# A decode kernel of four attention layers: how the transfers and products around a layer's end are ordered

What was changed: the head mapping of the backward layer was mended; the last two heads' rows of `wo` (`wol`) now load into the slot of `wo`'s third block; the five row parts of `wq` in layers 2 and 3 come in groups of 2, 2, 1 instead of 1, 2, 2; V28's products moved ahead of the last softmax; each of the last two heads is evicted in one activation instead of two.

## The chip, the cores and the metric

The kernel runs on one core of one Trainium2 chip. The metric is device time in microseconds (us). Layers are numbered 0 to 3, heads 0 to 31. Times inside a trace count from the span's start. Engines: PE is TensorE, PEld its weight loads, DVE VectorE, ACT ScalarE, SP the engine that issues the transfers. QT names PE's products with parts of `wq`, S the scores, YB the products with `wo`, TB a head's gather (the step that turns its evicted output into columns for `wo`).

## The reference

One token passes through four attention layers, with the weights and caches of A, B, A, B.

```python
for w in (A, B, A, B):           # D = 640, 32 heads, 8192 keys, head size 192, bf16
    q = layernorm(x) @ w.wq      # wq: 640 x 6144
    s = q_h . K_h * 192**-0.5    # K_h, V_h: 8192 x 192 for each head, 3.1 MB each
    o = softmax(s) . V_h
    x = x + concat(o) @ w.wo     # wo: 6144 x 640
```

Each K and V tile is used once per layer, so nearly all of the work is reading 848.4 MB.

## The kernel before

SBUF holds eight slots, each big enough for one K or V tile. A fixed `plan` lists all transfers; SP issues them in that order, and each waits until its slot's last user is done. `steps` is the program order of the computing engines.

```python
Q_PARTS = [[(0, 2), (2, 2), (4, 1)] if l < 2 else [(0, 1), (1, 2), (3, 2)] for l in range(NL)]
KEPT = {0: {("k", 0), ("v", 0)}, 1: {("v", 28), ("v", 29), ("v", 30), ("v", 31)}}   # reused two layers later
...
if l == 2 and p == 0:     # m: score products, s: softmax, v: V products, wq: columns of q
    part = [("m", l, 0), ("wq", l, 1), ("s", l, 0), ("v", l, 0), ("wq", l, 2)]   # ("wq", l, 0) is ahead
...
if p == H - 1:            # end of a layer
    part.append(("s", l, p))
    part += [("v", l, i) for i in range(H - AHEAD, H)]      # V28 to V31
    part.insert(-O_LAST, ("wc", l, 2))
...
plan.append(("wo", l, 2)); plan.append(("wol", l))          # wo's third block, then its last two heads
```

A K tile is multiplied by q in place on DVE, in four chunks; PE adds up the 192 columns with 24 matmuls of 512 columns, and only then is the slot free:

```python
for c in range(4):
    PE.wait(chunks[c])
    for r in range(QD // R):      # 6 matmuls per chunk
        ...matmul(S, lhsT=ident, rhs=k3[:, :, d0:d0 + R])
freed[nt] = ev_S[h] = e
```

The turn from layer 1 to layer 2: V28 to V31 of layer 1 and K0, V0 of layer 0 are kept there, so six of the eight slots are taken. The other two hold K31 and then `wq`'s first part, and `wo`'s third block and then `wq`'s second part. The third part waits until the first has been used; the next K tile, head 1 of layer 2, here called K1, waits until K0's scores are added up.

Of the kernel before, what the change touches and what calls it, by code (L numbers as in the profile page):

```python
# [63 lines left out]
HEADS_W = 10  # L64
# [3 lines left out]
AHEAD = 4  # L68
# [3 lines left out]
def build(nc, A_x, A_k, A_v, A_wq, A_wo, B_x, B_k, B_v, B_wq, B_wo, out):  # L72
# [13 lines left out]
    QW = H * DH  # L86
    Q_PARTS = [[(0, 2), (2, 2), (4, 1)] if l < 2 else [(0, 1), (1, 2), (3, 2)] for l in range(NL)]
    O_PART = [P] * NL
    OI = [O_LAST * DH // n for n in O_PART]
    NB = 3  # L90
    G = 4
# [6 lines left out]
    with ExitStack() as ctx:  # L98
# [14 lines left out]
        oT = sb("oT", [P, NW], BF16)  # L113
        oTl = sb("oTl", [P, max(OI)], BF16)
        o_sb = sb("o_sb", [P, 2 * DH], F32)
# [81 lines left out]
        for l in range(NL):  # L197
            if l < 2:
                plan.append(("wq", l, 0))
                steps += [("wq", l, g) for g in range(3)]  # L200
            elif l == 2:
                plan += [("wq", l, g) for g in range(3)]
                steps.append(("wq", l, 0))
            else:
                plan.append(("wq", l, 0))
                steps.append(("wq", l, 0))
            for p in range(H):
                if p in (HEADS_W, 2 * HEADS_W):
                    b = p // HEADS_W - 1
                    steps += [("wc", l, b), ("wo", l, b)]  # L210
                    plan.append(("wo", l, b))
                if first_load("k", l, p) == ("k", l, p):
                    plan.append(("k", l, p))
                if stays("k", l, p):
                    plan.append(("t", l, p))
                if l == 2 and p == 0:
                    part = [("m", l, 0), ("wq", l, 1), ("s", l, 0), ("v", l, 0), ("wq", l, 2)]
                elif p < H - AHEAD:
                    part = [("m", l, p), ("s", l, p), ("v", l, p)]
                else:  # L220
                    part = [("m", l, p)]
                    if p > H - AHEAD:
                        part.append(("s", l, p - 1))
                    if p == H - 1:
                        part.append(("s", l, p))
                        part += [("v", l, i) for i in range(H - AHEAD, H)]
                        part.insert(-O_LAST, ("wc", l, 2))
                steps += part
                plan += [n for n in part if n[0] == "v" and first_load(*n) == n]
                if l == 3 and p == 1:  # L230
                    for g in (1, 2):
                        plan.append(("wq", l, g))
                        steps.append(("wq", l, g))
            plan.append(("wo", l, 2))
            steps.append(("wo", l, 2))
            plan.append(("wol", l))
            steps.append(("wol", l))
        plan.append(("wob", NL - 1))
        at = {n: i for i, n in enumerate(steps)}

        def released(n):

            if n[0] in "kvt":
                l, p = n[1:]
                if n[0] != "t" and stays(*n):
                    l, p = n[1] + 2, ORDER[n[1] + 2]["heads"].index(head(*n[1:]))
                return at[("v" if n[0] == "v" else "m", l, p)]
            return at[n]
# [15 lines left out]
        for n in plan:  # L264
            if n[0] == "wol" and n[1] + 1 < NL:
                m = ("wq", n[1] + 1, 0)
                allot(m)
                before[n] = before[("wq", n[1] + 1, 2)] if n[1] == 0 else before[m]
            elif n[0] == "wob":
                before[n] = []  # L270
            elif n not in place:
                allot(n)
# [4 lines left out]
        def wq_rows(l, g):  # L277

            c0, k = Q_PARTS[l][g]
            if l < 2:  # L280
                i = place[("wq", l, 0)] * TS
                return pool[:, i + c0 * QW:i + (c0 + k) * QW].rearrange("p (c n) -> p c n", c=k)
            return slot[place[("wq", l, g)]][:, 0:k * QC].rearrange("p (c n) -> p c n", c=k)

        def wol_rows(l):

            if l + 1 == NL:
                i = place[("wol", l)] * TS
            else:
                i = place[("wq", l + 1, 0)] * TS + (DC * QW if l == 0 else QC)  # L290
            return pool[0:O_PART[l], i:i + OI[l] * D]

        def transfer(n):
# [4 lines left out]
            if n[0] == "wol":  # L298
                r0 = o["wol"] * DH
                if O_PART[l] == P:  # L300
                    return SP.op(lambda s: s.dma_start(
                        wol_rows(l), w["wo"][r0:r0 + O_LAST * DH].rearrange("(p i) n -> p (i n)", p=P)),
                        *free, sem=semOL, inc=16)
                k = O_PART[l] // O_LAST
                for h in range(O_LAST):
                    e = SP.op(lambda s, h=h: s.dma_start(
                        wol_rows(l)[h * k:(h + 1) * k],
                        w["wo"][r0 + h * DH:r0 + (h + 1) * DH].rearrange("(q e i) n -> e q (i n)", e=8, i=OI[l])),
                        *free, sem=semOL, inc=16)
                return e  # L310
            if n[0] == "t":
# [13 lines left out]
            elif n[0] == "wq":  # L325
                c0, k = Q_PARTS[l][n[2]]
                f = lambda s: s.dma_start(
# [52 lines left out]
        def layer(l, ev_z, ev_true):  # L380
# [36 lines left out]
            def q_columns(g):  # L417

                n = ("wq", l, g)
                c0, k = Q_PARTS[l][g]  # L420
                t3 = wq_rows(l, g)[:, :, ORDER[l]["q1"] if l < 2 else 0:]
# [16 lines left out]
            def q_spread(h):  # L438

                c0 = h * DH  # L440
                PE.wait(last["qT"], last["QB"], ev_const)
# [15 lines left out]
            def project(n, rows, o, ev_o):  # L457

                t3 = rows.rearrange("p (i n) -> p i n", n=D)
                k = t3.shape[1]  # L460
                end = n == ("wob", l) or n == ("wol", l) and l + 1 < NL
                PE.wait(ev_o, need(n), last["YB"])
                for i in range(k):
                    for c in range(DC):
                        e = PE.op(lambda t, i=i, c=c, f=y_first[0], fin=end and i == k - 1: t.matmul(  # L465
                            YB[:, c:c + 1], lhsT=t3[:, i, c:D:DC], rhs=o[:, i:i + 1], start=f, stop=fin,
                            skip_group_check=True), signal=(i == k - 1 and c == DC - 1), bank=use["YB"])
                        y_first[0] = False
                freed[n] = e
                return e  # L470
# [65 lines left out]
            def values(h):  # L536
# [16 lines left out]
                if h < H - O_LAST:  # L553
                    parts = [(o_sb[:], OB[par][:, 0:2 * DH])]
                else:
                    q = 1 if O_PART[l] == P else O_PART[l] // O_LAST // 8
                    parts = [(o_sb[:, i * DH:(i + 1) * DH].rearrange("p (i e q) -> p q e i", i=OI[l], q=q),
                              OB[par][:, i * DH:(i + 1) * DH].rearrange("p (q e i) -> p q e i", i=OI[l], q=q))
                             for i in range(2)]
                for o, i in parts:  # L560
                    ev_os[h] = AC.op(lambda a, o=o, i=i: a.activation(o, i, ACT.Copy, scale=rl[pi][:, 0:1]),  # L561
                                     e, ev_rl[h], last["osb"], bank=use[f"O{par}"])
                last["O"][par] = last["rl"][pi] = ev_os[h]

            def gather(h):
# [6 lines left out]
                last["osb"] = e  # L572
                o0 = (h % HEADS_W) * DH
                last["TO"] = last["row_written"] = AC.op(
                    lambda a: a.activation(orow[0:1, o0:o0 + DH], TB[0:1, C_O:C_O + DH], ACT.Copy), e, last["orow"], bank=use["TB"])  # L575

            def gather_last(h):

                n = O_PART[l] // O_LAST
                k = OI[l]  # L580
                r0 = (h - (H - O_LAST)) * n
# [14 lines left out]
            for i, n in enumerate(here):  # L596
# [15 lines left out]
                elif n[0] == "wc":  # L612
                    todo()
                    todo = None
                    columns(NW)
                    last["oTw"] = last["TT"]
                elif n[0] == "wo":
# [3 lines left out]
                    k = NW - NB if n == ("wo", NL - 1, 2) else NW  # L621
                    last["oT"] = project(n, slot[place[n]][:, 0:k * D], oT[:, 0:k], last["oTw"])
                else:
                    last["TT"] = last["TTn"]
                    last["oTl"] = ev_y = project(n, wol_rows(l), oTl[0:O_PART[l]], last["TTn"])
                    if l + 1 == NL:
                        ev_y = project(("wob", l), slot[place[("wo", l, 2)]][:, (NW - NB) * D:NW * D], oT[:, NW - NB:NW], last["oTw"])
                following = [m[2] for m in here[i + 1:] if m[0] == "m" and m[2] not in ev_q][:1]
# [68 lines left out]
```

## Time and profile before

| | before |
|---|---|
| device time | 1997.24 us median of 3 (1996.39 to 1998.24) |
| profiled span | 1994.7 us |
| read | 848.4 MB, mean 426 GB/s |
| a 3.1 MB tile follows the last in the stream after | 7.30 us |
| last V tile landed | 1983.18 us |

From the page of the kernel before: busy time, the shares in 40 slices, and the chain that ended last.

```profile
PE 1392.6 (70%) x10438; PEld 318.0 (16%) x7494; DVE 1047.4 (53%) x1074; ACT 220.3 (11%) x665; POOL 4.5 (0%) x22
...
DMA  9999999999999999999999999999999999999998
GB/s 410 431 431 428 432 429 429 430 431 430 428 430 431 428 432 428 431 429 429 431 382 431 428 431 428 431 430 429 431 429 427 430 430 429 430 429 429 429 432 345
...
q8 instruction: 70, 1.15, 0.2%
...
DMA 65%; PE 21%; DVE 12%; ACT 1%; issue 1%; another core or an unknown queue 0%; DVEq 0%
```

The kernel is bound by its transfers. Only the first, the last and slice 21 (382 GB/s) fall clearly below 430 GB/s. Slice 21 is the turn from layer 1 to layer 2. The stretches there, of the kernel before (columns: busy time and count of each engine, granted PE clock, DMA share, GB/s):

```profile
1013.00:1022.00 9.00, 6.88 (x146) 5.89 (x146) 0.35 (x4) 1.41 (x5) 0.00 (x0) 0.92 0.51 213
1022.00:1031.00 9.00, 7.21 (x62) 2.65 (x53) 6.36 (x12) 0.73 (x2) 0.54 (x1) 0.51 0.99 390
1031.00:1040.00 9.00, 8.14 (x137) 3.76 (x125) 2.66 (x5) 0.44 (x2) 0.00 (x0) 0.87 1.03 434
```

There is a hole from 1013 to 1022 us, where the mean DMA share is 0.51. The chain of waits of the kernel before through this stretch (start, us, what; a DMA line runs from a transfer's issue to its landing, the time that it stands in the queue included):

```profile
986.85 30.96 DMA pool<-in_B_wo_dram
1017.81 0.05 issue
1017.86 3.77 PE YB L465 x90
...
1025.52 1.77 DVE pool L495
1027.30 0.05 issue
1027.34 0.61 PE S L508
1027.95 6.42 PE S L58 x23
1034.37 2.23 PE QT L427 x90
...
1040.79 20.01 DMA pool<-in_A_k_cache_dram
```

Layer 2 starts when `wo`'s third block has landed, at 1017.8 us, and its products are done.

### The profile page before, as it was taken

Reading aid. Unit: us, or ns where it says so; the run is one execution under the profiler, and the core shown is the slowest. Engines: PE = TensorE matmul, PEld = TensorE weight load, DVE = VectorE, ACT = ScalarE, POOL = GpSimd, SP = SyncE. Lnnn points to the kernel's source line nnn. Section 1 sums busy time; section 2 is a strip of 40 time slices with the busy share of each in tenths; the row PEclk is TensorE's granted clock in tenths of the full one; section 3 lists DMA queues with packets and bytes.
Section 4 is the critical chain, followed back from the end, with each engine's and each line's share of the span. In section 5 each row is a group of like instructions: output and inputs, shape, how many; then the busy total and the mean of one; then the engine's idle time right before and its main releaser. Section 6 shows DMA issues by size and latency. Waiting matters only on the chain.

```text
span 1994.7 us, 20412 instructions
## 1 busy us (share of the span) xinstructions
PE 1392.6 (70%) x10438; PEld 318.0 (16%) x7494; DVE 1047.4 (53%) x1074; ACT 220.3 (11%) x665; POOL 4.5 (0%) x22
## 2 busy tenths in 40 slices
PE   4777777667567766767777676777776768767766
PEld 1111111111311111211031111111112212111112
DVE  3554554556255455455726545545663465554563
ACT  0111111110111111111011111111101111111111
POOL 0000000000000000000000000000000000000000
PEclk9888888887688888788878878887897888987889
DMA  9999999999999999999999999999999999999998
GB/s 410 431 431 428 432 429 429 430 431 430 428 430 431 428 432 428 431 429 429 431 382 431 428 431 428 431 430 429 431 429 427 430 430 429 430 429 429 429 432 345
DMA packets 40487, 849.67 MB, mean 426 GB/s; under 512 B 4688, under 2 KB 4688, under 8 KB 5328
## 3 DMA queue, kind: packets, MB, share of 16 engines
q1 hardware_dynamic: 40256, 848.38, 99.4%
q8 instruction: 70, 1.15, 0.2%
q14 instruction: 17, 0.14, 0.0%
q10 hardware_dynamic: 144, 0.00, 0.0%
HBM read 848.36 MB, written 0.00 MB: 425 GB/s over the span
## 4 chain that ended last, share of the span: by engine, by line
DMA 65%; PE 21%; DVE 12%; ACT 1%; issue 1%; another core or an unknown queue 0%; DVEq 0%
DMA pool<-in_B_k_cache_dram 32%; DMA pool<-in_A_k_cache_dram 30%; PE S L58 13%; DVE pool L495 10%; PE O L546 3%; DMA pool<-in_B_wo_dram 2%; PE TB L569 1%; DMA x_bf<-in_A_x_dram 1%; PE S L508 1%; PE YB L465 1%; DVE s_sb L516 1%; ACT p_sb L526 1%; PE QT L427 1%; PE TB L530 1%; DVE small L523 0%
## 5 line engine op out<-in xcount | busy, mean ns | idle before, releaser
L495 DVE TENSOR_TENSOR pool<-pool,q_sb 128x3072 bf16<-128x3072 bf16 x512 | 865.5, 1752 | 406.4 <-DMA pool<-in_A_k_cache_dram 208.3
L58 PE MATMUL S<-pool,ident 128*128 128x512 bf16 x2944 | 797.2, 425 | 35.1 <-DVE pool L495 34.9
L546 PE MATMUL O<-pool,p_sb 128*2 128x384 bf16 x4096 | 346.5, 420 | 1.4 <-DMA pool<-in_B_v_cache_dram 1.4
L508 PE MATMUL S<-pool,ident 128*128 128x512 bf16 x128 | 60.4, 472 | 225.7 <-DVE pool L495 225.5
L516 DVE TENSOR_REDUCE s_sb<-S 128x64 f32<-128x512 f32 x128 | 88.3, 690 | 229.1 <-PE S L58 229.1
L546 PEld LDWEIGHTS O<-pool,p_sb 128*2 128x2 bf16 x4096 | 128.0, 88 | 134.8 <-issue 98.4
L569 PE MATMUL TB<-o_sb,small 128*1 128x192 f32 x480 | 122.8, 389 | 38.2 <-DVE small L534 27.1
L453 ACT ACTIVATE q_sb<-QM 128x192 bf16<-128x192 f32 x120 | 39.6, 330 | 961.2 <-PE QM L446 961.2
L446 PEld LDWEIGHTS QM<-ident,qT 128*128 128x128 bf16 x240 | 23.1, 98 | 741.0 <-issue 725.6
L530 PE MATMUL TB<-small,ones 128*128 128x1 f32 x256 | 49.7, 263 | 109.9 <-ACT p_sb L526 109.9
L520 PE MATMUL QM<-ident,m_bf 128*128 128x128 bf16 x128 | 27.8, 217 | 122.9 <-DVE m_bf L519 121.2
L561 ACT ACTIVATE o_sb<-O,small 128x384 f32<-128x384 f32 (+1 forms) x136 | 77.2, 579 | 233.2 <-PE O L546 233.2
L534 DVE RECIPROCAL small<-TB 128x1 f32<-128x1 f32 x128 | 21.5, 168 | 122.4 <-PE TB L530 122.4
L526 ACT ACTIVATE p_sb<-s_sb,small 128x64 bf16<-128x64 f32 x128 | 44.5, 348 | 266.5 <-DVE small L523 266.5
L523 DVE TENSOR_REDUCE small<-QM 128x1 f32<-128x128 f32 x128 | 37.3, 291 | 62.3 <-PE QM L520 62.3
L575 ACT ACTIVATE orow<-TB 1x192 bf16<-1x192 f32 x120 | 38.3, 319 | 200.7 <-PE TB L569 200.7
L530 PEld LDWEIGHTS TB<-small,ones 128*128 128x128 f32 x256 | 38.9, 191 | 130.4 <-ACT p_sb L526 130.4
L508 PEld LDWEIGHTS S<-pool,ident 128*128 128x128 bf16 x128 | 12.7, 99 | 285.8 <-DVE pool L495 285.8
L520 PEld LDWEIGHTS QM<-ident,m_bf 128*128 128x128 bf16 x128 | 12.3, 96 | 215.3 <-ACT q_sb L453 126.9
L569 PEld LDWEIGHTS TB<-o_sb,small 128*1 128x1 f32 x480 | 33.5, 89 | 81.1 <-DVE small L534 36.0
L465 PE MATMUL YB<-oT,pool 128*128 128x1 bf16 x900 | 38.0, 178 | 5.1 <-DMA pool<-in_A_wo_dram 2.3
L465 PEld LDWEIGHTS YB<-oT,pool 128*128 128x128 bf16 x900 | 37.0, 131 | 5.9 <-ACT oT L479 2.9
(50 smaller groups left out, 215.4 us busy)
## 6 DMA issues: line engine op xcount, KB each, us to landing
pool<-in_B_k_cache_dram SPq DMA_DIRECT2D x64, 3072.0 KB, 35.5
pool<-in_A_k_cache_dram SPq DMA_DIRECT2D x63, 3072.0 KB, 27.6
pool<-in_A_v_cache_dram SPq DMA_DIRECT2D x63, 3072.0 KB, 33.3
pool<-in_B_v_cache_dram SPq DMA_DIRECT2D x60, 3072.0 KB, 37.2
pool<-in_A_wo_dram SPq DMA_DIRECT2D x6, 2400.0 KB, 24.0
pool<-in_B_wo_dram SPq DMA_DIRECT2D x5, 2400.0 KB, 33.3
pool<-in_A_wq_dram SPq DMA_DIRECT2D x1, 7680.0 KB, 20.8
pool<-in_B_wq_dram SPq DMA_DIRECT2D x1, 7680.0 KB, 29.3
```

The source lines that it names most:

```text
L58: return t.add_instruction(mybir.InstMatmult(name=t.bass.get_next_instruction_name(), engine=mybir.EngineType.PE, ins=[t.lower_ap(rhs), t. ...
L453: lambda a: a.activation(q_sb[i][:], QM[:, 0:DH], ACT.Copy), e, last["q"][i], bank=use["QM"])
L465: e = PE.op(lambda t, i=i, c=c, f=y_first[0], fin=end and i == k - 1: t.matmul(YB[:, c:c + 1], lhsT=t3[:, i, c:D:DC], rhs=o[:, i:i + 1], s ...
L495: e = DV.op(lambda v, d0=d0: v.tensor_tensor(k3[:, :, d0:d0 + QD], kin[:, :, d0:d0 + QD], q_sb[qi][:, d0:d0 + QD].unsqueeze(1).broadcast_t ...
L508: t.matmul(S[:, :], lhsT=ident[:], rhs=k3[:, :, d0:d0 + R], start=True, stop=fin) if d0 == 0 else
L516: ev_s = DV.op(lambda v: v.tensor_reduce(s_sb[par][:], S[:].rearrange("p (j r) -> p j r", r=R), AX.X, ALU.add), ev_S[h], last["s"][par], b ...
L520: e = PE.op(lambda t: t.matmul(QM[:, C_MX:C_MX + P], lhsT=m_bf[par][:, 0:1].broadcast_to([P, P]), rhs=ident[:], start=True, stop=True), ev ...
L526: ev_p[h] = AC.op(lambda a: a.activation(p_sb[pi][:], s_sb[par][:], ACT.Exp, bias=negm[par][:, 0:1], accum_out=l_col[par][:]), ev_n, ev_s, ...
L530: e = PE.op(lambda t: t.matmul(TB[:, C_L + par:C_L + par + 1], lhsT=ones[:, 0:1].broadcast_to([P, P]), rhs=l_col[par][:], start=True, stop ...
L546: e = PE.op(lambda e, g=g, j=j, f=m < G, fin=fin: e.matmul(OB[par][32 * g:32 * g + 2, 0:2 * DH], lhsT=p_sb[pi][:, j:j + 2], rhs=t[:, j * D ...
L561: ev_os[h] = AC.op(lambda a, o=o, i=i: a.activation(o, i, ACT.Copy, scale=rl[pi][:, 0:1]), e, ev_rl[h], last["osb"], bank=use[f"O{par}"])
L569: e = PE.op(lambda t, i=i: t.matmul(TB[0:1, C_O:C_O + DH], lhsT=pick[:, i:i + 1], rhs=o_sb[:, i * DH:(i + 1) * DH], start=(i == 0), stop=( ...
```

## The change

The intent: queue more bytes before the hole, shorten the end of a layer, and free `wol` from a wait. The core of the diff:

```diff
-    Q_PARTS = [[(0, 2), (2, 2), (4, 1)] if l < 2 else [(0, 1), (1, 2), (3, 2)] for l in range(NL)]
+    Q_PARTS = [(0, 2), (2, 2), (4, 1)]
-    NB = 3
+    NB = 7                      # rows of wo's third block loaded late (wob) in the last layer
...
-                        part.append(("s", l, p))
-                        part += [("v", l, i) for i in range(H - AHEAD, H)]
-                        part.insert(-O_LAST, ("wc", l, 2))
+                        part += [("v", l, p - 3), ("s", l, p), ("v", l, p - 2), ("wc", l, 2), ("v", l, p - 1), ("v", l, p),
+                                 ("wo", l, 2)]
...
         def wol_rows(l):
+            return slot[place[("wo", l, 2)]][:, NW * D:(NW + OI) * D]
...
-                c0 = h * DH
+                c0 = head(l, h) * DH - ORDER[l]["q1"] + Q_FIRST * DH
...
-                freed[n] = e
+                if n != ("wo", l, 2):
+                    freed[("wo", l, 2) if n[0] == "wol" else n] = e
...
-                o0 = (h % HEADS_W) * DH
+                o0 = (head(l, h) - ORDER[l]["wo"][h // HEADS_W]) * DH
```

The mended mapping concerns layer 3, whose heads run in another order. By reading the code, the old one took the wrong head's columns of q and the wrong rows of `wo` there. The comparison with the reference does not see it. It only changes offsets.

## The prediction

> **What bounds it now.** The 40-slice table shows DMA at 9 tenths throughout, 426 GB/s mean. DVE (53%) and PE (70%) have slack; the chain of waits is 65% DMA. Completions show a 3.1 MB tile every 7.30 us, so 848.4 MB need about 1969 of 1994.7 us. 25 us are not stream: about 3 of start, the tail after the last V tile (1983.2 to 1994.7; the stream ends at 1990.1), engine skew, and one hole. Bandwidth falls in slice 21 (382 GB/s): at the turn from layer 1 to layer 2 1 us windows show 0.8 to 0.08 DMA share from 1013 to 1022.

> **What the change does.** Bytes and, but for wob, the order of transfers are unchanged. The mended head mapping only changes column offsets: no time.
> (a) wq for layers 2 and 3 in 2, 2, 1 row parts instead of 1, 2, 2: 1.47 MB (3.4 us) more is queued before the hole.
> (b) V28's products before the last softmax: they ran 1001.1 to 1003.8, after it; the end chain shortens by 1.5 to 2.5 us.
> (c) The last two heads' eviction is one activation (about 0.58 us) instead of two (0.94): 0.7 us per layer end.
> (d) wol lives in wo's slot: it no longer waits, but wo's slot is freed 0.7 us later. wob grows from 3 to 7 rows and goes before wol.

> **How much is on the critical path.** Less than the hole looks. A transfer ends with the slowest of 16 engines ([...]the 16 increments of wq's first part spread from 1014.2 to 1022.4). That slowest engine hardly idled: part two landed 9.2 us after part one, against 6.9 elsewhere. So (a) plus (b) can win at most 2.3 us there, not the 5.5 us of lost bandwidth. Part is given back: the doubled first part lands near 1025.8 instead of 1022.4, PE now waits for it before layer 2's first score matmuls, so K0's slot is freed about when it was (1034.4; 1033.5 to 1035), and the next K tile's issue becomes the limit. Net there: 1 to 2.3 us. The turns 0 to 1 and 2 to 3 have full DMA windows: nothing is won. In layer 3's tail only (c) counts, 0.3 us, since the last V tile's landing decides.

> **Predicted:** 1995.1 us, 80% range 1992.3 to 1997.6. Faster by over 2%: 0.005, within 2%: 0.99, slower: 0.005.

> **What the profile would show.** Right: slice 21 above 395 GB/s; wq's first part lands 3.4 us later, its second at most 1 us later than before; PE's first QT group waits for DMA at about 1022 to 1026; the first K tile after the wq parts lands 1 to 2.3 us earlier; the last V tile lands by as much earlier; tail 0.3 us shorter. Wrong: that K tile's issue moves past 1036 (PE at half clock, as it was from 1021 to 1030), so nothing is won; or before 1032, and over 3 us are won.

> **What would make it wrong.** The skew hides more: if instruction fetches (70 packets in the DMA queue table, about 1.07 us each on one engine) fall on other engines, the slowest engine's lag at the end (8.2 us) changes by a microsecond either way. A new hole at the 2 to 3 turn, K0 landing 3.4 us later there. Run to run spread is 1.9 us, near the effect.

## The result, and the profile after

| | before | after |
|---|---|---|
| median, 4 runs each | 1997.22 us (1996.39 to 1998.24) | 1998.57 us (1996.90 to 1999.30) |
| ratio after to before | | 1.0005, 95% interval 0.9988 to 1.0023 |
| profiled span | 1994.7 us | 1997.5 us |

Ratios here are the comparison of runs of the same rounds, with a 95% interval; they are not quite the ratio of the medians quoted. The two kernels are not told apart by time; the predicted gain is not there, and the median lies above the predicted range (1992.3 to 1997.6).

From the page of the changed kernel:

```profile
PE 1391.7 (70%) x10438; PEld 320.6 (16%) x7494; DVE 1047.7 (52%) x1074; ACT 220.0 (11%) x657; POOL 4.5 (0%) x22
...
GB/s 410 430 432 428 430 430 429 431 430 429 429 430 431 429 429 431 428 431 430 430 368 430 431 430 428 430 431 430 430 429 427 429 429 430 429 431 429 429 432 336
```

Slice 21 fell to 368 GB/s instead of rising. The same stretches of the changed kernel:

```profile
1013.00:1022.00 9.00, 6.89 (x127) 5.47 (x115) 0.43 (x5) 1.08 (x2) 0.00 (x0) 0.50 0.79 332
1022.00:1031.00 9.00, 7.14 (x103) 3.56 (x98) 6.46 (x9) 0.73 (x2) 0.54 (x1) 0.50 0.98 372
1031.00:1040.00 9.00, 8.14 (x111) 2.48 (x92) 2.33 (x4) 0.44 (x2) 0.00 (x0) 0.81 0.72 254
```

The first hole is half filled (213 became 332 GB/s), and a new one opened from 1031 to 1040 us (434 became 254). The chain of waits of the changed kernel through this stretch:

```profile
997.18 28.96 DMA pool<-in_A_wq_dram
1026.15 0.05 issue
1026.20 2.56 PE QT L411 x90
1028.76 0.45 PE S L492
1029.21 7.57 PE S L58 x23
1036.78 2.23 PE QT L411 x90
...
1042.16 20.27 DMA pool<-in_A_k_cache_dram
```

The chain no longer begins with `wo` but with `wq`'s first part. That part is now twice as large and lands at 1026.15 us; PE has to work through it (90 one-column matmuls, 2.56 us) before it gets to K0's scores. In order of time, PE of the kernel before (the bracket is the idle time ahead and what ended it):

```profile
1024.83 1.39 PE L427 MATMUL QT<-xb,pool 128*128 128x1 bf16 x45
1027.34 0.61 PE L508 MATMUL S<-pool,ident 128*128 128x512 bf16 x1 [1.13 <-DVE pool L495]
1027.74 6.63 PE L58 MATMUL S<-pool,ident 128*128 128x512 bf16 x23
```

and of the changed kernel:

```profile
1026.20 2.56 PE L411 MATMUL QT<-xb,pool 128*128 128x1 bf16 x90 [1.34 <-DMA pool<-in_A_wq_dram]
1028.62 0.59 PE L492 MATMUL S<-pool,ident 128*128 128x512 bf16 x1
1029.00 7.78 PE L58 MATMUL S<-pool,ident 128*128 128x512 bf16 x23
```

The score matmuls start 1.28 us later and take over a microsecond longer. K1 is issued at 1036.81 instead of 1034.40 us, and lands at 1047.82 instead of 1046.19 us. (The transfer that ends both chains above is a later one, head 2's K tile.) K1's issue, in the kernel before and in the changed one:

```profile
1034.40 0.34 SPq L322 DMA_DIRECT2D pool<-in_A_k_cache_dram  x1
1036.81 0.34 SPq L306 DMA_DIRECT2D pool<-in_A_k_cache_dram  x1
```

From there on the stream is full (427 to 432 GB/s in every slice after slice 21 but the last), and the last V tile lands 1.66 us later too (1984.84 against 1983.18 us): the delay of K1, carried to the end.

Two readings of the records recur below. First, each transfer leaves 16 completions in the records; "lands" is the last of them, and the lag is the time from the first to the last, up to 8.3 us in the kernel before and 8.6 us in the changed one. The page counts 16 DMA engines, so one completion is read here as one engine's share, the last as the slowest engine's; the records do not name the engine. Second, PE's granted clock is 1.0 or 0.5 in the records of both kernels. In the changed kernel it was 0.5 until 1034.4 us, in the kernel before only until 1030.8. The starts of the 24 score matmuls are 0.43 us apart at half clock and 0.22 us apart at full clock in both traces (on average 0.427 and 0.216).

Of the 2.41 us by which K1 was issued later, an estimate from these spacings: with the kernel before's clock release at 1030.8, matmuls started at 1028.6 would have made 5 at half clock and 19 at full, to about 1035.0, so 0.6 us is the later start and 1.8 us the later clock release.

### The profile page after: what moved, and what is told of

Its sections match the earlier page's. It is cut to its first block, busy times and chain, and to the rows that moved or that the text cites. A ratio compares the mean times of both kernels' runs of the same rounds, so it can differ in the third digit from the quotient of the medians.

```text
span 1997.5 us, 20396 instructions
## 1 busy us (share of the span) xinstructions
PE 1391.7 (70%) x10438; PEld 320.6 (16%) x7494; DVE 1047.7 (52%) x1074; ACT 220.0 (11%) x657; POOL 4.5 (0%) x22
## 4 chain that ended last, share of the span: by engine, by line
DMA 66%; PE 19%; DVE 13%; ACT 1%; issue 1%; another core or an unknown queue 1%; DVEq 0%
DMA pool<-in_B_k_cache_dram 32%; DMA pool<-in_A_k_cache_dram 30%; PE S L58 12%; DVE pool L479 11%; PE O L530 2%; DMA pool<-in_A_wo_dram 2%; DMA pool<-in_A_wq_dram 1%; DMA x_bf<-in_A_x_dram 1%; PE TB L549 1%; PE S L492 1%; PE QT L411 1%; ACT p_sb L510 1%; PE TB L514 1%; DVE s_sb L500 1%; PE YB L448 1%
## 5 line engine op out<-in xcount | busy, mean ns | idle before, releaser
L530 PE MATMUL O<-pool,p_sb 128*2 128x384 bf16 x4096 | 342.0, 416 | 4.9 <-DMA pool<-in_B_v_cache_dram 4.2
L543 ACT ACTIVATE o_sb<-O,small 128x384 f32<-128x384 f32 x128 | 77.1, 602 | 231.7 <-PE O L530 231.7
```

Source lines behind the costliest of these rows:

```text
L530: e = PE.op(lambda e, g=g, j=j, f=m < G, fin=fin: e.matmul(OB[par][32 * g:32 * g + 2, 0:2 * DH], lhsT=p_sb[pi][:, j:j + 2], rhs=t[:, j * D ...
L543: lambda a: a.activation(o, i, ACT.Copy, scale=rl[pi][:, 0:1]), e, ev_rl[h], last["osb"], bank=use[f"O{par}"])
```

## The experiments

**Theory 1.** The doubled first part of `wq` moves the hole instead of filling it: PE waits for its landing, K0's slot is freed late, K1 is issued late, and K1's landing decides the end. Nothing was won at the end of layer 1, since `wo`'s landing gates it. **Rivals:** 2, `wol` in `wo`'s slot frees that slot late; 3, the moved V28 or the single eviction costs it; 4, it is the PE clock.

### wq back to 1, 2, 2

```diff
-    Q_PARTS = [(0, 2), (2, 2), (4, 1)]
+    Q_PARTS = [[(0, 2), (2, 2), (4, 1)] if l < 2 else [(0, 1), (1, 2), (3, 2)] for l in range(NL)]
```

> The changed kernel with only the wq row parts of layers 2 and 3 put back to 1, 2, 2. Theory 1 (the doubled first part moves the hole: PE waits for its landing at about 1026.2, layer 2's first score matmuls end late, and the next K tile is issued at 1036.8 instead of 1034.4): that K tile is issued at 1033.8 to 1034.8 and lands (last of 16 completions) at 1045.7 to 1046.7, as in the kernel before; the trace span falls by 1 to 2 us below that of the changed kernel. Rival 2 (wol in wo's slot frees that slot later, and this delays everything after): the K tile still lands after 1047.3. Either theory: time within 0.15% of the kernel before.

Measured: 1997.04 us median of 5, ratio 0.9998 to before (0.9985 to 1.0010). K1 was issued at 1034.03 and landed at 1046.09 us, and the span was 1995.0 us, 2.5 below that of the changed kernel (1 to 2 were expected). Rival 2 falls: `wol` was still in `wo`'s slot. So does rival 3: V28's new place and the single eviction were still in.

### Only wq at 2, 2, 1, in the kernel before

The doubled part fills its slot, so `wol` of layers 1 and 2 has to go to `wo`'s slot as well.

```diff
-    Q_PARTS = [[(0, 2), (2, 2), (4, 1)] if l < 2 else [(0, 1), (1, 2), (3, 2)] for l in range(NL)]
+    Q_PARTS = [[(0, 2), (2, 2), (4, 1)] for l in range(NL)]
...
+            if l in (1, 2):
+                i = place[("wo", l, 2)] * TS + NW * D
```

> The kernel before with only the wq parts at 2, 2, 1 (which forces wol of layers 1 and 2 into wo's slot, since the first part's slot is now full). Theory 1: the first K tile after the wq parts is issued at 1036 to 1037.5 and lands at 1047 to 1048.5, as in the changed kernel, though V28's order and the evictions are those of before. Rival 3 (the loss comes from V28's products ahead or from the single eviction): it lands at 1045.7 to 1046.7.

Measured: 1997.39 us median of 5, ratio 1.0000 (0.9987 to 1.0012). K1 was issued at 1034.97 and landed at 1046.86 us: between the two expected bands, a miss for both. The chain is that of the changed kernel all the same:

```profile
997.50 28.10 DMA pool<-in_A_wq_dram
1025.61 0.05 issue
1025.65 2.56 PE QT L433 x90
1028.21 0.45 PE S L515
1028.66 6.28 PE S L58 x23
```

PE's wait and the score start (1028.08 us) came with the 2, 2, 1 split alone, without V28's new place and without the single eviction. The clock was released at 1031.2 us, near the 1030.8 of the kernel before, and so only 0.57 us of issue time was lost, close to the 0.6 estimated above. The split alone costs about 0.6 us, not 2.4.

### The changed kernel again

> The changed kernel once more, unchanged, for how much its landmarks move by themselves. Theory 4 (the TensorE clock steps on a grid of about 3.41 us [...], and at half clock the score matmuls of layer 2's first tile take 427 instead of 216 ns each): the score matmuls start at about 1028.5 again, but the K tile's issue moves with the clock's release, anywhere in 1034.5 to 1037, near 1033 + half of (release - 1027). Rival: it is issued at 1036.8 within 0.3 again. Time within 0.15% of before.

### PE kept busy while it waits

```diff
+                if l == 2 and g == 0:
+                    PE.wait(last["QT"], ev_const)
+                    for i in range(14):
+                        PE.op(lambda t: t.matmul(QT[:, 256:384], lhsT=ident[:], rhs=ident[:], start=True, stop=True), ...)
```

> The changed kernel with 14 idle 128-column matmuls (about 1.5 us at half clock) on PE before it waits for wq's first part in layer 2, so that PE is busy from about 1023 on. Theory 4 (the half clock, granted from 1007 to 1034 in the changed kernel, is what stretches layer 2's first score matmuls past 1036): the clock is released about 3.4 us or more earlier, the score matmuls end by 1035, the K tile is issued by 1035 and lands by 1046.3. If the wait for wq's landing alone does it: issue stays at 1036.3 or later, landing at 1047.3 or later.

The 3.4 us there equals one step of the clock's grid in the traces (3.41); that a busy PE brings the release forward was the assumption, which no trace had shown.

Measured: 1997.88 us median of 4, ratio 1.0002 (0.9988 to 1.0015). The idle matmuls filled the wait (1024.85 to 1026.3 us, some 0.5 us past `wq`'s landing at 1025.84), but the clock was released at 1032.5, no earlier than in the unfilled repeat. K1 was issued at 1036.0 and landed at 1046.82 us. Both expectations missed: the clock was no earlier, yet K1 was issued and landed a little before the bands of the wait alone. This filler did not bring the clock forward. In eleven traces the release came 3.1 to 5.9 us after the first 512-column score matmul. In the changed kernel's first trace PE had by then worked without a break for 8.2 us (from 1026.20 us, first on the 90 one-column matmuls). What the release goes by was not shown.

### What the hole is worth: one kept tile less

```diff
-KEPT = {0: {("k", 0), ("v", 0)}, 1: {("v", 28), ("v", 29), ("v", 30), ("v", 31)}}
+KEPT = {0: {("k", 0), ("v", 0)}, 1: {("v", 28), ("v", 29), ("v", 30)}}
```

> The kernel before, keeping only V28 to V30 of layer 1 for layer 3, not V31: one slot is free at the turn from layer 1 to layer 2, so the hole closes, and one more 3.1 MB tile is read (7.3 us). If the hole costs only what the slowest DMA engine loses (2.3 to 3 us by the completions): 4 to 5.5 us slower than before. If it costs the bandwidth lost there (5.5 us): 1 to 2.5 us slower.

Measured: 2001.99 us median of 5, ratio 1.0021 (1.0008 to 1.0035), which is 4.3 us by the medians; the last V tile landed 4.5 us later in the trace (1987.66 us). The hole nearly closed (mean DMA share 0.90 from 1013 to 1022 us, 0.51 before), and the last completions of `wq`'s parts came 6.92 us apart: the slowest engine had no hole left. One tile more costs 7.3 us, so closing the hole gave back about 2.8 us (7.3 less 4.5). The hole is worth 2.8 us, not the 5.5 us of lost bandwidth. The prediction had this right: in the kernel before, the 16 completions of `wq`'s first part ran from 1014.2 to 1022.4 us, so most of the "lost" bandwidth is engines that had run ahead. The end of the stream shows the same: the first completion of the last V tile came only 1.58 us later than before (1976.58 against 1975.00), its last one 4.48 us later, a lag of 11.1 us. The engine that was ahead won most of the lost bandwidth back, the slowest 2.8 us, and a tile has landed only with the slowest.

### An earlier start of layer 2

If `wo`'s landing sets layer 2's start, less work after that landing should move it. The third block was loaded as 8 and 7 rows in all layers, and the first 8 rows' products put ahead of V31's gather.

```diff
-            if l + 1 == NL:
-                plan.append(("wob", l))
-                steps.append(("wob", l))
+            plan.append(("wob", l))
+            steps.append(("wob", l))
...
-                    if todo is not None:
+                    if todo is not None and n[2] != 2:     # V31's gather after the first 8 rows
```

With `wq` at 1, 2, 2:

> The changed kernel with wq at 1, 2, 2, and with the split of the third wo block (8 rows, then 7 rows as a second transfer) in all four layers, the first 8 rows' products done before V31's gather. Theory 1, second half (layer 2's start is set by the landing of wo's third block at 1017.6 plus 3.9 us of its products, so that neither V28's order nor the eviction could win anything): the products end at 1019.6 to 1020.4 instead of 1021.4, the second wq part is issued 1 to 1.8 us earlier than 1021.1, the slowest DMA engine loses 1 us less, the next K tile lands 1 to 2.8 us earlier than 1046.1; the tail after the last V tile is 0.3 to 0.8 us shorter than the changed kernel's. Time 0.05 to 0.2% below before. Rival (something else sets layer 2's start): K tile lands at 1046 or later.

and at 2, 2, 1:

> The same split with wq at 2, 2, 1 as in the changed kernel. Theory 1: the earlier end of layer 1 buys nothing here, since PE waits for the doubled first part, which lands at about 1025.8 as before: the K tile is issued at 1034.5 to 1037 and lands at 1046 to 1048, 1.5 us or more after that of the kernel with 1, 2, 2. Rival (the order of parts hardly matters once the layer ends sooner): the two K tiles land within 0.7 us of each other.

Measured on the same chip in the same rounds: 1996.91 us (1996.25 to 1997.59) with 1, 2, 2 and 1998.69 us (1997.65 to 1999.61) with 2, 2, 1, medians of 5 each; ratios to before 0.9998 (0.9985 to 1.0010) and 1.0006 (0.9994 to 1.0019). The two sets of five do not overlap; their means differ by 1.67 us. The chain of the 1, 2, 2 kernel:

```profile
986.76 28.21 DMA pool<-in_B_wo_dram
1014.97 0.05 issue
1015.02 1.77 PE YB L447 x40
1016.78 1.37 PE TB L564 x12
1018.16 2.11 PE YB L447 x50
...
1026.57 7.04 PE S L58 x23
1033.62 2.23 PE QT L410 x90
```

Its `wo` products end at 1020.26 us, `wq`'s second part is issued at 1020.28 (0.84 earlier than with 1, 2, 2 alone, short of the expected 1 to 1.8), and K1 lands at 1045.21 us, the earliest of the ten traces in the table below, 0.88 us before that of 1, 2, 2 alone (expected 1 to 2.8); the expected 0.05 to 0.2% of total time was missed too (0.02%). With 2, 2, 1 the products ended at 1020.64 us, PE idled 2.13 us for `wq`'s first part, K1 was issued at 1036.09 and landed at 1047.13 us. That agrees with both halves of theory 1: what sets layer 2's start is `wo`, and with the doubled first part an earlier start buys nothing. After the last V tile the result was ready 8.35 us later, 0.6 less than in the changed kernel (8.96), as expected, but hardly less than in the kernel before (8.41); and the output's own transfer then took 3.6 us from issue to landing (2.5 before, 3.1 in the changed kernel). Why that varies stays open.

### A plain eviction

```diff
-                    o, i = (o_sb[:].rearrange("p (h i e) -> p h e i", h=2, i=OI),
-                            OB[par][:, 0:2 * DH].rearrange("p (h e i) -> p h e i", h=2, i=OI))
+                o, i = o_sb[:], OB[par][:, 0:2 * DH]
...
-lhsT=o_sb[:, i * DH + c * n:i * DH + (c + 1) * n]
+lhsT=o_sb[:, i * DH + c:(i + 1) * DH:k]
```

> The split with 1, 2, 2, and with the last two heads' eviction as one plain contiguous activation; the gather then loads its weights with a stride of three elements. If the reordered read is what holds the single eviction at 0.91 us (two took 0.94): the activation takes 0.58 us and the gather's 12 matmuls take as long as before, so the tail after the last V tile is another 0.3 us shorter. If the stride slows the weight load: the gather grows past 1.0 us at full clock.

Measured: 1996.84 us median of 5, ratio 0.9998 (0.9985 to 1.0012). The activation took 0.58 instead of 0.91 us, and the gather's 12 matmuls took 1.22 us at full clock instead of 0.86: the 0.33 us moved from one to the other, and the result was ready 8.36 us after the last V tile, as without it.

### The first group as two transfers

Same bytes ahead of the hole as in the changed kernel, but PE can use the first row part while the second lands.

```diff
+    Q_PARTS[2] = [(0, 1), (2, 2), (4, 1), (1, 1)]
...
+                plan += [("wq", l, g) for g in (0, 3, 1, 2)]
+                steps += [("wq", l, 0), ("wq", l, 3)]
```

> The split kernel with the plain eviction, and with 2.9 MB of wq queued ahead of the hole as in the changed kernel, but as two transfers of one row part each into the one slot, each with its own wait, so that PE works on the first while the second lands. If the changed kernel lost its gain to PE's wait for the doubled first part (theory 1): layer 2's first score matmuls start at 1027 to 1027.6 instead of 1028.1 to 1028.8, the K tile is issued at 1033.5 to 1035 and lands at 1043.8 to 1045.2, no later than in the split with 1, 2, 2 (1045.2 to 1045.5) and 1.4 us or more earlier than in the changed kernel (1046.6 to 1047.8). If only the order of bytes counts: it lands at 1046.4 or later as with 2, 2, 1. Time 0 to 0.2% below before.

Measured: 1997.22 us median of 5, ratio 1.0000 (0.9986 to 1.0013). The score matmuls started at 1027.25 us, as expected, but the clock was released only at 1032.7, K1 was issued at 1035.32 and landed at 1046.57 us, past every band that theory 1 gave and inside the rival's (1046.4 or later, "only the order of bytes counts"). So PE's wait for a doubled part is not all of it: without that wait, too, the bytes moved ahead won nothing. With half clock until 1032.7, 24 matmuls from 1027.25 on end near 1035 by the spacings above. `wq`'s last part landed at 1036.75 us here, so a full stream would have landed K1 at 1044.05; in the traces with `wq`'s parts moved ahead K1 lands 10.8 to 11.9 us after its issue, so, as an estimate, those matmuls would have had to end by about 1033. How much of this run's loss is the clock's late release stays open: no run set that release.

### Instruction fetches

The prediction named instruction fetches as a risk, and the lag between DMA engines was large (8.18 us at the last V tile). The page of the kernel before shows 70 packets of instructions, 16 KB each; by the trace one takes 1.06 us on average, which the page's 0.2% of 16 engines' span counts as one engine's time. Its 10438 matmuls and 7494 weight loads make 256 to a packet; by that ratio the 5120 added below make 20 more. To see whether the fetches make the lag, 20 idle matmuls per head were added to the kernel before.

```diff
                 PE.wait(need(nv_), ev_p[h], last["O"][par])
+                for i in range(20):
+                    PE.op(lambda t: t.matmul(OB[par][:, 400:401], lhsT=ident[:], rhs=ident[:, 0:1], start=True, stop=True), ...)
```

> The kernel before with 20 idle one-column matmuls per head, 2560 in all with as many weight loads, in places where PE has slack: about 20 more instruction fetches of 16 KB (70 in the kernel before). If each fetch holds one DMA engine for about 1.07 us and so makes the slowest engine's lag (8.2 us over the first of the 16 completions of the last V tile): 88 to 92 packets, a lag of 9.5 to 11.5 us there, and 1.5 to 3.5 us more time. Rival (the lag has another cause): lag 7.5 to 8.8, time within 1 us of before.

From the page of this kernel:

```profile
PE 1501.7 (75%) x12998; PEld 394.6 (20%) x10054; DVE 1047.3 (52%) x1074; ACT 220.3 (11%) x665; POOL 4.5 (0%) x22
...
q8 instruction: 90, 1.47, 0.3%
```

That is 256 matmuls and weight loads to a packet again.

Measured: 2012.67 us median of 5, ratio 1.0075 (1.0063 to 1.0088), far more than expected. Most of that is not the fetches: `wq`'s second part landed 8.6 us later and the stretch from the last V tile to the output's landing grew from 11.1 to 19.0 us, as the added matmuls stand in PE's program order at the layers' ends. So the time tells nothing about fetches, and the lag at the last V tile (8.5 us, expected 9.5 to 11.5) does not either, since at the turn from layer 2 to layer 3 the engines drew partly level (the lag fell from 5.4 to 3.9 us, where in the kernel before it rose from 3.6 to 5.0). What counts is the stretch before the first hole. V31 of layer 1 had its first completion at 1003.63 us (1003.80 before), its last at 1014.16 (1012.10 before): the lag rose from 8.30 to 10.53 us with 43 instead of 34 fetches up to there. That agrees with fetches making the slowest engine late (9 more fetches, 2.23 us more lag); which engine a fetch used is not in the records.

### All traces together

From the records of starts, clock and completions; us, K1 as issued and as landed, V31 the last V tile as landed.

```
kernel             wq      scores start  clock released  K1 issued  K1 landed  V31 landed  V31 - K1
split, 1,2,2       1,2,2   1025.97       1030.6          1033.65    1045.21    1982.34     937.13
split, plain       1,2,2   1025.88       1031.7          1034.12    1045.47    1982.67     937.20
after, 1,2,2       1,2,2   1026.81       1030.6          1034.03    1046.09    1983.31     937.22
before             1,2,2   1027.34       1030.8          1034.40    1046.19    1983.18     936.99
split, two         1+1,2,1 1027.25       1032.7          1035.32    1046.57    1983.82     937.25
after, again       2,2,1   1028.16       1032.5          1035.68    1046.62    1983.61     936.99
after, filler      2,2,1   1028.79       1032.5          1036.00    1046.82    1983.92     937.10
before, 2,2,1      2,2,1   1028.08       1031.2          1034.97    1046.86    1983.45     936.59
split, 2,2,1       2,2,1   1028.59       1032.9          1036.09    1047.13    1984.25     937.12
after              2,2,1   1028.62       1034.4          1036.81    1047.82    1984.84     937.02
```

The last column is the same within 0.7 us in ten traces. What happens up to K1 decides when the stream ends. All kernels with the plain 1, 2, 2 land K1 by 1046.2 us, all with more queued ahead at 1046.5 or later.

What K1 waits for is not the same in the two groups. With 1, 2, 2, `wq`'s last part landed at 1038.51 us in the kernel before and K1 7.69 us after it; in the other three K1 came 7.31 to 7.32 us after that part: the stream was full, or nearly, and K1's own issue cost little or nothing. With more queued ahead, `wq`'s last part landed 1.5 to 2.1 us earlier than before (1036.42 to 1037.03), but K1 only 9.8 to 10.8 us after it. There the stream stood and waited for K1's issue.

## Why the prediction was wrong

- **What bounds the kernel, and that the hole is worth far less than its bandwidth:** right. Predicted at most 2.3 us instead of 5.5; the run with one kept tile less gives 2.8.
- **"The end chain shortens by 1.5 to 2.5 us" through V28's place, and 0.7 us through the single eviction:** wrong as far as it should reach layer 2. V28's products did run at 998.4 to 999.8 instead of 1001.1 us, but layer 2's `wo` products started at 1017.67 instead of 1017.86 us, since `wo`'s third block lands at 1017.6 to 1017.8 in both. The eviction took 0.91 us, not 0.58: its reordered read is what costs, as the plain variant shows.
- **`wq`'s first part lands near 1025.8 and PE waits for it:** right (1026.15 us, a wait of 1.34 us).
- **"K0's slot is freed about when it was (1034.4; 1033.5 to 1035)" and "Net there: 1 to 2.3 us":** this is the step that failed. K1 was issued at 1036.81 and, in the repeat, at 1035.68 us, and landed 1.63 and 0.43 us later than before, not 1 to 2.3 earlier. The branch named as wrong ("that K tile's issue moves past 1036", with PE at half clock) is what the first trace showed. The bytes moved ahead did their part: `wq`'s last part landed 1.48 us earlier than before (1037.03 against 1038.51), 2.09 in the repeat. But K1 then came 10.80 us after it instead of 7.69. Even with K0's slot freed at 1034.97 us, in the kernel before at 2, 2, 1, nothing was won. The step was wrong in its sum as well: K1 took 10.8 to 11.9 us from issue to landing in the traces with more queued ahead, so a slot freed at 1034.4 would, as an estimate, land it at 1045.2 to 1046.3: at best 1.0 us earlier than before. With the bytes moved ahead, K1 itself has to be issued earlier than before, and it hangs on layer 2's start, which had not moved.
- **`wq`'s second part at most 1 us later:** it landed 1.69 us later (1033.27), 1.02 in the repeat.
- **Tail 0.3 us shorter:** wrong. The result was ready 8.96 us after the last V tile landed, against 8.41. In the trace the gather of V31 ran at half clock; PE of the kernel before:

```profile
1983.22 2.73 PE L546 MATMUL O<-pool,p_sb 128*2 128x384 bf16 x32 [1.41 <-DMA pool<-in_B_v_cache_dram]
1987.00 0.86 PE L585 MATMUL TB<-small,o_sb 128*64 128x1 f32 x12 [1.05 <-ACT o_sb L561]
```

  and of the changed kernel:

```profile
1984.88 2.73 PE L530 MATMUL O<-pool,p_sb 128*2 128x384 bf16 x32 [3.50 <-DMA pool<-in_B_v_cache_dram]
1988.63 1.44 PE L565 MATMUL TB<-small,o_sb 128*64 128x1 f32 x12 [1.02 <-ACT o_sb L543]
```

  With the gather at full clock in the run with `wq` at 1, 2, 2 (0.86 us) the same tail took 8.43 us: nothing gained, nothing lost.
- **The turns 0 to 1 and 2 to 3 give nothing:** in agreement. K1's delay of 1.63 us in the trace is that of the last V tile, 1.66.

The expected gain was thus not lost to a cost of the new parts. It was turned into a new wait: the bytes moved ahead landed earlier, but the next link (K0's scores, then K1's issue) came no earlier, or later, and the stream stood until it did. How the lateness of that link divides between PE's wait for `wq` and the clock is estimated here, not shown. Not settled: whether the changed kernel is slower at all. Its mean lies above that of before in both sets of rounds (by 1.07 and 0.57 us), but both intervals of the ratio include 1; only the split pair (1.67 us between 1, 2, 2 and 2, 2, 1) is told apart, and there the new order is the slower one. The split with 1, 2, 2 has the lowest medians (1996.91 and 1996.84 us), but against before it is not resolved either.

## What to carry to other kernels

When a hole in the transfers comes from slots that are all taken, queueing more bytes ahead of it helps only if the release of the next slot moves as well; follow the chain of waits through the hole and ask which link the added bytes lengthen (here K1 came 10.80 instead of 7.69 us after `wq`'s last part). Work that ends before the landing which the chain goes through can be shortened for nothing (here V28's products, 2.7 us earlier, for 0.19 us at the start of `wo`'s products). A gain of a microsecond is better read from landmarks in the traces (issue and landing of one transfer) than from total times, and the same program should be traced twice before a difference is given a cause.
